# A third PSUM bank for the cross products of batch 0, 33 rows of bias, and the last two units ahead of the splits

## The chip, the cores and the metric

The kernel runs on one core of a Trainium2 chip. Its time is device microseconds of one execution; a comparison uses the median of several. Before the change the median of 3 runs is 2718.03 us (2716.43 to 2720.4). The engines are called PE (TensorE), DVE (VectorE), ACT (ScalarE), POOL (GpSimd) and SP (SyncE, which here only issues DMAs). PSUM is the memory that PE writes its results to; this kernel divides it into eight banks of 128 x 512 float32.

## What is computed

A spectral layer (a real Fourier transform along the sequence, a complex linear map with a soft threshold, the inverse transform) and then a feed-forward layer on all 8 x 3008 rows:

```python
X = np.fft.rfft(x, axis=1)                    # x is (8, 3008, 256)
Yr = Xr @ w_r - Xi @ w_i + b_r
Yi = Xr @ w_i + Xi @ w_r + b_i
lam = 0.01
Yr = np.sign(Yr) * np.maximum(np.abs(Yr) - lam, 0.0)
Yi = np.sign(Yi) * np.maximum(np.abs(Yi) - lam, 0.0)
y = np.fft.irfft(Yr + 1j * Yi, n=3008, axis=1)
h = y.reshape(8 * 3008, 256) @ w_in           # (256, 2048)
out = (h - np.tanh(h)) @ w_out                # (2048, 256)
```

## The kernel before

**The transforms.** The length 3008 is 64 x 47, so a transform is two stages of matmuls. Forward: `Forward` (a chunk of 4 of the 32 row pairs) computes the 47-point stage and writes its result to a DRAM tile `a`; `Spectrum` (a pair of the 24 frequency columns, 12 pairs a batch) reads `at` back, does the 64-point stage (`transform`), the complex product with the linear weights (`cross`), the soft threshold and the first inverse stage (`inverse`), and writes `zo` to a DRAM tile `z` (`put`). `Chunk` (5 row pairs, 470 columns) reads `zin` back from `z`, does the second inverse stage (`time`, in two halves) and the feed-forward layer in 16 steps, `up` (tiles `h`, `th`, `g`, `gh`, `gl`) and `down` (`o`). To keep float32 precision most matmuls are done on a high and a low part (`split`), three products each.

**Batch 0 is done alone.** Nothing of the feed-forward layer can start until batch 0's `z` is there, so batch 0 has a version of its own, with whole float32 matmuls in place of three products: `WholeSpectrum`, whose twelve instances are the `units` u0 to u11. A unit's steps:

- `dft`: the 64-point stage on PE (L288) and ACT's copy `xf` (L360). `sum`: `sf` on DVE (L365).
- `cross`: three pairs of matmuls on PE. Two go to `vv` (`ps_v`), behind a matmul that puts the biases there (`ones` by `brow`, 33 rows, L370); the third, the part that both results share, goes to `t1` (`ps_t`).
- `common`: ACT copies `t1` to `tb` (L380). `shrink`: DVE adds `tb` and `vv` to `y` in four pieces (L333), ACT does one side of the threshold (`up`, L385), DVE the other (`mn`, L387). `join`: DVE adds the two (L391).
- `inverse`: PE's matmul to `pz` (L395). `put`: ACT's copy `zo` (L350) and the DMA of `z`.

In the loop over the units, iteration i does the `dft` of unit i, `cross` of unit i-1, `common`, `shrink` and `join` of unit i-2, and `inverse` and `put` of unit i-3. Beside them it loads the weights of the feed-forward layer, which come in float64, and converts them on DVE, ACT and POOL (`convert`, a list `ops` of which each iteration takes some), and reads the constant `i2t` of the second inverse stage. The chunks of batch 1's forward transform that follow (`following`, four of them) and `time` of the first two feed-forward chunks are written out by hand behind the loop.

**What sets the order.** All of this stands in a `manual_schedule` for the five engines: each engine executes its instructions in the order in which the code issues them, and waits at each for what it needs. Behind it come the feed-forward steps, one slot each; a plan (`put`, `plan_forward`, `plan_spectrum`) sets into which slot a step of the next batch's transforms goes.

**PSUM.** The pool `ps_h` has two banks (`h`, and in the units' part `ps_v`), `ps_o` two (tags `o0` and `o1`, in the units' part `ps_t1`), `ps_f` four for the rest. A tile can be written when the tile that had the bank before it has been read. `keep_warm` issues matmuls on zeros to a tile `idle` of `ps_h`, which nothing reads; it is called with 8 at the start and with 16 ahead of the units.

**Bias.** `load_linear` loads the two weight matrices and the tile `bias`, each bias row to all 128 partitions. `combine_linear` makes `brow` from 33 of its rows; `bias` itself is read again in batches 1 to 7 (L322).

Of the kernel before, what the change touches and what calls it, by code (L numbers as in the profile page):

```python
# [10 lines left out]
F32 = mybir.dt.float32  # L11
# [5 lines left out]
B, S, D, FF = 8, 3008, 256, 2048  # L17
# [51 lines left out]
def spectral_ffn(ctx, tc, x, w_r, w_i, b_r, b_i, w_in, w_out, f1, f2, i1, i2, out):  # L69
    nc = tc.nc  # L70
    P = 128
# [8 lines left out]
    const = ctx.enter_context(tc.tile_pool(name="const", bufs=1))  # L80
    load = ctx.enter_context(tc.tile_pool(name="load", bufs=2))
    work = ctx.enter_context(tc.tile_pool(name="work", bufs=2))
# [24 lines left out]
    def load_linear():  # L107
        wr = ffn.tile([P, 2, D], F32, name="wr_f", tag="g_h")
        wi = load.tile([P, 2, D], F32, name="wi_f", tag="at", bufs=3)
        nc.sync.dma_start(out=wr, in_=w_r.rearrange("(t p) e -> p t e", p=P))  # L110
        nc.sync.dma_start(out=wi, in_=w_i.rearrange("(t p) e -> p t e", p=P))
        bias = const.tile([P, 2, D], F32, name="bias")
        for k, v in enumerate((b_r, b_i)):
            nc.sync.dma_start(out=bias[:, k, :], in_=v.rearrange("(o e) -> o e", o=1).to_broadcast([P, D]))
        return wr, wi, bias

    def combine_linear(wr, wi, bias, zero):
        w2 = ffn.tile([P, 2, D], F32, name="w2_f", tag="g_h")
        w3 = ffn.tile([P, 2, D], F32, name="w3_f", tag="g_h")
        nc.vector.scalar_tensor_tensor(out=w3, in0=wr, scalar=-1.0, in1=wi, op0=ALU.mult, op1=ALU.subtract)  # L120
        nc.gpsimd.tensor_tensor(out=w2, in0=wi, in1=wr, op=ALU.subtract)
        ones = work.tile([33, P], F32R, name="ones", tag="s_l")
        nc.vector.tensor_scalar(out=ones, in0=zero[:33, :P], scalar1=1.0, scalar2=None, op0=ALU.add)
        top = work.tile([33, 2 * D], F32R, name="bias_top", tag="tmp", bufs=4)
        flat = bias[:33].rearrange("o r e -> o (r e)")
        nc.scalar.copy(out=top, in_=flat)  # L126
        brow = work.tile([33, 2 * D], F32R, name="brow", tag="ot", bufs=1)
        nc.vector.tensor_copy(out=brow, in_=zero[:33])
        nc.vector.tensor_copy(out=brow[0:1], in_=top[0:1].bitcast(F32))
        nc.vector.tensor_tensor(out=brow[32:33], in0=flat[32:33], in1=top[32:33].bitcast(F32), op=ALU.subtract)  # L130
        return (wr, w2, w3), (ones, brow)
# [136 lines left out]
    class Spectrum:  # L268
# [79 lines left out]
        def put(self, pz):  # L348
            zo = work.tile([P, 512], F32, name="zo", tag="tmp", bufs=4)
            nc.scalar.copy(out=zo, in_=pz)  # L350
            nc.sync.dma_start(out=z_rows(z_dram[self.b], self.jp), in_=zo)

    class WholeSpectrum(Spectrum):
        def temp(self, name, tag):
            return ffn.tile([P, 2, D], F32, name=name, tag=tag)
# [9 lines left out]
            nc.vector.tensor_tensor(out=self.sf, in0=pr[:, :, 0, :], in1=self.xf[:, :, 1, :], op=ALU.add)  # L365

        def cross(self):
            self.vv = ps_h.tile([P, 512], F32, name="ps_v", tag="h")
            ones, brow = bias_rows
            nc.tensor.matmul(self.vv, ones, brow, start=True, stop=False)  # L370
            self.t1 = ps_o.tile([P, 512], F32, name="ps_t1", tag=f"o{self.jp % 2}")
            for k, (dst, lhs) in enumerate((
                (self.vv[:, :D], self.xf[:, :, 1]), (self.vv[:, D:], self.xf[:, :, 0]), (self.t1[:, :D], self.sf),
            )):
                for t in range(2):
                    nc.tensor.matmul(dst, lhs[:, t], whole_lin[2 - k][:, t, :], start=k == 2 and t == 0, stop=k > 0 and t == 1)

        def common(self):
            self.tb = work.tile([P, D], F32, name="tb0", tag="xi")
            nc.scalar.copy(out=self.tb, in_=self.t1[:, :D])  # L380

        def shrink(self):
            y = self.add(lambda jj, ri: self.tb[jj * 64:(jj + 1) * 64, :])
# [94 lines left out]
    def plan_forward(b, start, each, ahead, first=0):  # L478
        for ch in range(first, NP // XC):
            f = Forward(b, ch)  # L480
            put(start + ch * each - ahead, f.load)
            for q in range(XC // 2):
                put(start + ch * each + q * each // 2, f.part, q)

    def plan_spectrum(b, start, each, ahead, lag):
        for jp in range(NJ // 2):
            s = Spectrum(b, jp)
            at = start + jp * each
            put(at - ahead, s.load)
            put(at, s.dft)  # L490
            put(at + lag, s.cross, 0)
            put(at + lag + 1, s.cross, 1)
            put(at + lag + 2, s.shared)
            put(at + 2 * lag + 3, s.inverse)
# [5 lines left out]
    chunks = [Chunk(c) for c in range(NCH)]  # L500
# [6 lines left out]
    with tc.manual_schedule(engines={E.PE, E.Activation, E.DVE, E.Pool, E.SP}):  # L507
# [6 lines left out]
        def keep_warm(n):  # L514
            for _ in range(n):
                nc.tensor.matmul(idle, warm[:, :P], warm, start=True, stop=True)
# [14 lines left out]
                f, q = steps[i - 1]  # L531
                f.keep(q, nc.vector.tensor_copy if i % 2 == 0 else nc.scalar.copy)
        lin_in = load_linear()
        bias = lin_in[2]
        keep_warm(16)
        units = [WholeSpectrum(0, jp) for jp in range(NJ // 2)]
        for u in units[:3]:
# [6 lines left out]
        raws, ops = [], []  # L544
# [10 lines left out]
        def unit(i):  # L555
            return units[i] if 0 <= i < NU else None

        for i in range(NU + 1):
            if unit(i - 2):
                unit(i - 2).common()  # L560
            if unit(i):
# [14 lines left out]
            if i < len(where):  # L576
# [2 lines left out]
                    nc.sync.dma_start(out=i2t[:, :10 * 94], in_=i2[:, :10 * 94])  # L579
                if i % 2:  # L580
                    ops += convert([(k // 4, k % 4, raws[k]) for k in (i - 1, i)])
            if i == 7:
                nc.sync.dma_start(out=i2t[:, 10 * 94:], in_=i2[:, 10 * 94:])
            if i in (8, 9):
                following[i - 8].load()
            if 3 <= i < 6:
                split_lin(i - 3)
            for op in ops[:(0, 0, 2, 2, 2, 2, 2, 3, 3, 3, 3, 2, 0)[i]]:
                op()
                ops.remove(op)  # L590
            if i in (11, 12):
                following[0].split(i - 11)
        assert not ops
        u10, u11 = units[-2:]
        LATE = 80
        following[2].load()
        for c in range(2):
            chunks[c].load(0, LATE)
        u10.inverse()
        for q in range(2):  # L600
            following[0].dft(q)
        u11.common()
        u11.shrink()
        u10.put(u10.pz)
        u11.join()
        u11.inverse()
        following[1].split(0)
        following[0].keep(0, nc.vector.tensor_copy)
        u11.put(u11.pz)
        for c in range(2):  # L610
            chunks[c].load(LATE, 96)
        following[0].keep(1)
        following[3].load()
        following[1].dft(0)
        following[1].split(1)
        following[1].keep(0, nc.vector.tensor_copy)
        following[1].dft(1)
        following[2].split(0)
        following[1].keep(1)
        following[2].dft(0)  # L620
        following[2].split(1)
        following[2].keep(0, nc.vector.tensor_copy)
        following[2].dft(1)
        for t in range(2):
            chunks[0].time(t)
        following[2].keep(1)
        for q in range(2):
            following[3].split(q)
            following[3].dft(q)
            following[3].keep(q, (nc.scalar.copy, nc.vector.tensor_copy)[q])  # L630
        for t in range(2):
            chunks[1].time(t)

    for i in range(2):
        put(2 * i - 2, ffn_weights, 1, 2 + i)
    for i in range(8):
        put(1 + 8 * i // 3, ffn_weights, 2 + i // 4, i % 4)
    plan_forward(1, 8, 2, 3, LOOK)
    plan_spectrum(1, 31, 4, 7, 2)
    for b in range(2, B):  # L640
        end = NF * (next(c for c in range(NCH) if begin[c] + sizes[c] > b * NP) - 1)
        plan_forward(b, end - 104, 2, 3)
# [48 lines left out]
```

## Time and profile before

| what | us |
|---|---|
| median of 3 runs | 2718.03 |
| the profiled execution's own time | 2716.88 |
| its span | 2715.1 |
| PE busy | 2679.6 |
| DVE busy | 1733.3 |
| ACT busy | 1380.0 |
| POOL busy | 56.6 |

The span runs from the first instruction to the last of one profiled execution; the time has 1.8 us around it. From 200 to 2500 us PE is idle for 1.6 us in all; the first 200 us hold batch 0 and the first feed-forward steps. In the views below, a row of a timeline is: start in us, duration in us, engine, line, operation, the tile written and the tiles read, with a count where several of one kind follow each other, and in brackets the idle time of the engine ahead of it and what ended it. A row of the chain that ended last is start, duration and what.

### The profile page before, as it was taken

How to read it: one execution, taken by the hardware profiler on the slowest of the kernel's cores; microseconds unless marked ns; L12 is line 12 of the kernel's file. 1: busy time of each engine (PE TensorE's matmuls, PEld its weight loads, DVE VectorE, ACT ScalarE, POOL GpSimd, SP SyncE). 2: the span in 40 equal slices, each digit the busy share in tenths (PEclk: the TensorE clock that was granted, in tenths of full speed). 3: DMA queues.
4: the chain of work that ended last, by engine and by line, in shares of the span. 5: the costliest groups of instructions: out<-in, count | busy, mean ns of one | idle time of the engine just before them, and what ended most of it. 6: DMA issues, size and time to landing. Idle time of an engine off the chain costs nothing.

```text
span 2715.1 us, 36888 instructions
## 1 busy us (share of the span) xinstructions
PE 2679.6 (99%) x14112; PEld 2385.1 (88%) x14112; DVE 1733.3 (64%) x3041; ACT 1380.0 (51%) x2591; POOL 56.6 (2%) x47
## 2 busy tenths in 40 slices
PE   8799999999999999999999999999999999999999
PEld 5579888999889998899988999899988999998989
DVE  5786776766556666567665666656675667655555
ACT  3584455444554455545455454645446444444445
POOL 2130000000000000000000000000000000000000
PEclk9899999999999999999999999999999999999999
DMA  7532114111131113211023110311104111100000
GB/s 209 154 110 66 46 59 118 42 49 36 41 110 49 38 36 101 70 46 49 28 58 101 38 53 31 107 59 46 48 24 121 45 42 40 35 22 22 20 19 17
DMA packets 105217, 163.58 MB, mean 60 GB/s; under 512 B 7440, under 2 KB 71056, under 8 KB 104944
## 3 DMA queue, kind: packets, MB, share of 16 engines
q1 hardware_dynamic: 105040, 161.22, 19.8%
q8 instruction: 111, 1.82, 0.3%
q14 instruction: 66, 0.54, 0.1%
HBM read 86.22 MB, written 74.97 MB: 59 GB/s over the span
## 4 chain that ended last, share of the span: by engine, by line
PE 92%; DVE 4%; ACT 1%; DMA 1%; issue 1%; POOL 0%; SPq 0%; DVEq 0%; ACTq 0%; POOLq 0%
PE o L460 37%; PE h L439 36%; PE ps_v L308 4%; PE ps_i L426 4%; PE ps_f L288 3%; PE ps_t L308 2%; DVE y L333 1%; PE ps_f L236 1%; PE ps_f L238 1%; PE ps_f L237 1%; PE ps_i L344 1%; PE ps_i L345 1%; PE ps_i L343 1%; DVE g L444 0%; DMA a<-st 0%
## 5 line engine op out<-in xcount | busy, mean ns | idle before, releaser
L444 DVE TENSOR_TENSOR g<-h,th 128x470 f32<-128x470 f32 (+1 forms) x832 | 531.7, 639 | 560.5 <-ACT th L442 552.7
L442 ACT ACTIVATE th<-h 128x470 f32<-128x470 f32 (+1 forms) x832 | 462.9, 557 | 768.4 <-PE h L439 768.2
L448 DVE TENSOR_TENSOR gl<-g,gh 128x470 fp32r<-128x470 f32 (+1 forms) x832 | 533.2, 641 | 289.2 <-ACT gh L446 203.3
L446 ACT CAST gh<-g 128x470 fp32r<-128x470 f32 (+1 forms) x832 | 482.8, 580 | 390.5 <-DVE g L444 382.3
L460 PE MATMUL o<-gh,wout_l 128*128 128x470 f32 (+1 forms) x1664 | 632.4, 380 | 1.4 <-ACT gh L446 1.3
L460 PE MATMUL o<-gl,wout_h 128*128 128x470 f32 (+1 forms) x1664 | 616.5, 371 | 3.5 <-DVE gl L448 3.4
L460 PE MATMUL o<-gh,wout_h 128*128 128x470 f32 (+1 forms) x1664 | 615.7, 370 | 0.0
L439 PE MATMUL h<-yh,win_l 128*128 128x470 f32 (+1 forms) x1664 | 481.5, 370 | 4.3 <-DVE g L444 3.8
L439 PE MATMUL h<-yl,win_h 128*128 128x470 f32 (+1 forms) x1664 | 480.7, 370 | 0.0
L439 PE MATMUL h<-yh,win_h 128*128 128x470 f32 (+1 forms) x1664 | 480.6, 370 | 0.0
L460 PEld LDWEIGHTS o<-gl,wout_h 128*128 128x128 f32 x1664 | 312.9, 188 | 45.1 <-DVE gl L448 6.4
L439 PEld LDWEIGHTS h<-yh,win_l 128*128 128x128 f32 x1664 | 310.7, 188 | 41.8 <-DVE g L444 4.7
L460 PEld LDWEIGHTS o<-gh,wout_l 128*128 128x128 f32 x1664 | 313.0, 188 | 36.5 <-issue 1.8
L439 PEld LDWEIGHTS h<-yh,win_h 128*128 128x128 f32 x1664 | 311.0, 188 | 35.6
L439 PEld LDWEIGHTS h<-yl,win_h 128*128 128x128 f32 x1664 | 310.9, 188 | 35.6
L460 PEld LDWEIGHTS o<-gh,wout_h 128*128 128x128 f32 x1664 | 313.5, 188 | 32.0
L333 DVE TENSOR_TENSOR y<-tb,ps_v 64x256 f32<-64x256 f32 x384 | 160.0, 417 | 13.0 <-ACT tb L380 9.0
L426 PEld LDWEIGHTS ps_i<-i,zin 96*128 96x128 f32 x1024 | 128.3, 194 | 4.4 <-issue 1.3
L426 PE MATMUL ps_i<-i,zin 96*128 96x94 f32 x1024 | 130.0, 275 | 0.6 <-DMA zin<-z 0.6
L288 PEld LDWEIGHTS ps_f<-f,at 128*128 128x128 f32 x768 | 101.1, 192 | 13.8 <-issue 8.8
L288 PE MATMUL ps_f<-f,at 128*128 128x128 f32 x768 | 102.8, 276 | 6.2 <-ACT bias_top L126 6.2
L94 DVE TENSOR_TENSOR x_l<-xt,x_h 94x512 fp32r<-94x512 f32 x112 | 78.6, 708 | 46.4 <-ACT x_h L93 46.3
(102 smaller groups left out, 2102.3 us busy)
## 6 DMA issues: line engine op xcount, KB each, us to landing
xt<-in_x SPq DMA_DIRECT2D x64, 384.0 KB, 3.7
at<-a SPq DMA_DIRECT2D x96, 256.0 KB, 2.8
z<-zo SPq DMA_DIRECT2D x96, 256.0 KB, 2.4
out<-ot SPq DMA_DIRECT2D x50, 470.0 KB, 3.0
a<-st SPq DMA_DIRECT2D x56, 384.0 KB, 3.2
zin<-z SPq DMA_DIRECT2D x42, 480.0 KB, 4.1
w_raw<-in_moe_w_in SPq DMA_DIRECT2D x8, 512.0 KB, 4.3
w_raw<-in_moe_w_out SPq DMA_DIRECT2D x8, 512.0 KB, 3.9
```

What stands on the lines that cost most here:

```text
L94: rest.tensor_tensor(out=lo, in0=src, in1=hi.bitcast(F32), op=ALU.subtract)
L236: nc.tensor.matmul(pv, f1h, xl, start=True, stop=False)
L288: nc.tensor.matmul(pv[:, t, jj], self.at[:, jj, t * P:(t + 1) * P], rhs, start=True, stop=True)
L308: nc.tensor.matmul(dst, lhs[:, t], rhs[:, t, :], start=n == 0, stop=n == 5)
L333: nc.vector.tensor_tensor(out=y[ri * 64:(ri + 1) * 64, jj, :], in0=common(jj, ri), in1=self.vv[jj * 64:(jj + 1) * 64, ri * D:(ri + 1) * D] ...
L426: nc.tensor.matmul(ps[:, k * 94:(k + 1) * 94], self.zt[:, k, t * P:(t + 1) * P], i2t[:, p * 94:(p + 1) * 94], start=True, stop=True,)
L439: nc.tensor.matmul(h[:, :n], lhs[:, t, f * P:(f + 1) * P], rhs[:, t, :n], start=k == 0, stop=k == 5)
L442: nc.scalar.activation(out=th[:, :n], in_=h[:, :n], func=AF.Tanh)
L444: nc.vector.tensor_tensor(out=g[:, :n], in0=h[:, :n], in1=th[:, :n], op=ALU.subtract)
L446: nc.scalar.copy(out=gh[:, :n], in_=g[:, :n])
L448: nc.vector.tensor_tensor(out=gl[:, :n], in0=g[:, :n], in1=gh[:, :n].bitcast(F32), op=ALU.subtract)
L460: nc.tensor.matmul(self.o[t][:, :n], lhs[:, f, t * P:(t + 1) * P], rhs[:, :n], start=f == 0 and k == 0, stop=f == NF - 1 and k == 2,)
```

## The change

- `load_linear` loads the bias rows to 33 partitions only, as a tile `bias_rows` that `combine_linear` reads. The tile `bias` for 128 partitions is loaded later, by `load_bias(bias, P)` behind the loop.
- `vv` of every third unit (u2, u5, u8, u11) comes from the bank `o1`. `t1` of two units shares one tile, in two halves of the bank `o0`.
- The loop ends one iteration earlier, and what is left of u9, u10 and u11 is written out: `shrink`, `cross`, `join`, `inverse` and `put` of these stand ahead of the splits of `following[0]`, with a `keep_warm(7)` between them. The weight conversions that are left over (`ops`) stand behind `dft` and `keep` of `following[1]`.
- The second part of `i2t` is loaded there and not in iteration 7. The `dft` of `following[2]` stands behind `time` of the first feed-forward chunk.
- In the plan for batch 1, the forward chunks start at slot 12 and not 8, the spectra at 35 and not 31, with 11/3 slots each and not 4.

The built programs differ in the banks as well as in the order. `idle` is written again by `keep_warm(7)`, so it has its bank of `ps_h` until then, and the units' `ps_v` have one bank of `ps_h` and `o1`: u0 and u1 the bank of `ps_h`, u2 `o1`, u3 and u4 the bank of `ps_h`, u5 `o1`, and so on. Before, the `ps_v` have both banks of `ps_h` in turn, and `ps_t` both of `ps_o`.

PE's rows in iterations 8 and 9, with the engines that a row's first instruction waits for, before (`ps_v` of u7 is the first of them, `ps_t_617` is its `t1`, `ps_i_625` is the inverse of u5, `ps_f_644` the dft of u9, and the last row is `ps_v` of u8):

```order
L370 MATMUL ps_v<-brow,ones 128x512 [waits DVE_49,PE_49]
L376 MATMUL ps_v<-w_f,xf 128x256 [waits Activation_49]
L376 MATMUL ps_v<-w_f,xf 128x256 x3
L376 MATMUL ps_t_617<-wr_f,sf 128x256 [waits DVE_49]
L376 MATMUL ps_t_617<-wr_f,sf 128x256
L395 MATMUL ps_i_625<-mn,i_f 128x512 [waits DVE_49,PE_49]
L288 MATMUL ps_f_644<-f_131,at 128x2x64 [waits DMAHW3_49,PE_49]
L288 MATMUL ps_f_644<-f_131,at 128x2x64 x3
L370 MATMUL ps_v<-brow,ones 128x512 [waits DVE_49,PE_49]
```

And the same place now:

```order
L378 MATMUL ps_v<-brow,ones 128x512 [waits DVE_49,PE_49]
L386 MATMUL ps_v<-w_f,xf 128x256 [waits Activation_49]
L386 MATMUL ps_v<-w_f,xf 128x256 x3
L386 MATMUL ps_t_569<-wr_f,sf 128x256 [waits Activation_49]
L386 MATMUL ps_t_569<-wr_f,sf 128x256
L405 MATMUL ps_i_621<-mn,i_f 128x512
L291 MATMUL ps_f_640<-f_131,at 128x2x64 [waits DMAHW3_49]
L291 MATMUL ps_f_640<-f_131,at 128x2x64 x3
L378 MATMUL ps_v<-brow,ones 128x512
```

The order is the same; the waits moved. `ps_v` of u7 waits for DVE in both: before for y of u5, now for y of u6, which had the bank. `ps_v` of u8 (last row) waits for DVE before and for nothing now. `t1` of u7 waits now for ACT, which copies `t1` of u6 out of the same bank.

ACT's rows at the end of the units, before (the first `zo` is that of u8, `tb_775` is of u10, `tb_821` of u11, the last `zo` is that of u11):

```order
L350 COPY zo<-ps_i_760 128x512
L187 CAST win_h<-w_f 128x512 x2
L93 CAST x_0_0_h<-xt 94x512
L380 COPY tb_775<-ps_t_752 128x256
L385 ACTIVATE up<-y,column 128x512
L350 COPY zo<-ps_i_796 128x512
L93 CAST x_0_1_h<-xt 94x512
L380 COPY tb_821<-ps_t_788 128x256
L385 ACTIVATE up<-y,column 128x512
L350 COPY zo<-ps_i_811 128x512
L93 CAST x_1_0_h<-xt 94x512
L350 COPY zo<-ps_i_836 128x512
```

And now (`tb_760` is of u10, `tb_782` of u11):

```order
L353 COPY zo<-ps_i_755 128x512
L390 COPY tb_760<-ps_t_747 128x256
L395 ACTIVATE up<-y,column 128x512
L390 COPY tb_782<-ps_t_747 128x256
L353 COPY zo<-ps_i_780 128x512
L395 ACTIVATE up<-y,column 128x512
L353 COPY zo<-ps_i_796 128x512
L93 CAST x_0_0_h<-xt 94x512
L93 CAST x_0_1_h<-xt 94x512
L353 COPY zo<-ps_i_813 128x512
```

The two casts `win_h` and the splits of `following[0]` and `following[1]` (`x_0_0_h` to `x_1_0_h`) stood between the steps of u10 and u11; now only the two of `following[0]` stand there, ahead of the last `zo`.

PE's rows around `time` of the first feed-forward chunk (`ps_i_889`, `ps_i_897`), before:

```order
L236 MATMUL ps_f_883<-x_2_1_l,f_h 96x512
L237 MATMUL ps_f_883<-x_2_1_h,f_l 96x512
L238 MATMUL ps_f_883<-x_2_1_h,f_h 96x512
L426 MATMUL ps_i_889<-i_265,zin 128x94 x5
L426 MATMUL ps_i_897<-i_265,zin 128x94 x5
L439 MATMUL h<-yh,win_l 128x470 x2
```

And now:

```order
L436 MATMUL ps_i_875<-i_266,zin 128x94 x5
L436 MATMUL ps_i_883<-i_266,zin 128x94 x5
L449 MATMUL h<-yh,win_l 128x470 x2
L449 MATMUL h<-yh,win_h 128x470 x2
L449 MATMUL h<-yl,win_h 128x470 x2
L239 MATMUL ps_f_895<-x_2_0_l,f_h 96x512
L240 MATMUL ps_f_895<-x_2_0_h,f_l 96x512
L241 MATMUL ps_f_895<-x_2_0_h,f_h 96x512
```

The forward stage of `following[2]` (`x_2_0`, `x_2_1`) stood ahead of `time`; it now stands behind the first `h`.

The diff:

```diff
@@ -109,12 +109,15 @@
         nc.sync.dma_start(out=wi, in_=w_i.rearrange("(t p) e -> p t e", p=P))
-        bias = const.tile([P, 2, D], F32, name="bias")
+        rows = load_bias(work.tile([33, 2, D], F32, name="bias_rows", tag="tmp", bufs=4), 33)
+        return wr, wi, rows
+
+    def load_bias(dst, n):
         for k, v in enumerate((b_r, b_i)):
-            nc.sync.dma_start(out=bias[:, k, :], in_=v.rearrange("(o e) -> o e", o=1).to_broadcast([P, D]))
-        return wr, wi, bias
-
-    def combine_linear(wr, wi, bias, zero):
+            nc.sync.dma_start(out=dst[:, k, :], in_=v.rearrange("(o e) -> o e", o=1).to_broadcast([n, D]))
+        return dst
+
+    def combine_linear(wr, wi, rows, zero):
         w2 = ffn.tile([P, 2, D], F32, name="w2_f", tag="g_h")
@@ -122,7 +125,7 @@
         top = work.tile([33, 2 * D], F32R, name="bias_top", tag="tmp", bufs=4)
-        flat = bias[:33].rearrange("o r e -> o (r e)")
+        flat = rows.rearrange("o r e -> o (r e)")
         nc.scalar.copy(out=top, in_=flat)
@@ -350,6 +353,8 @@
+    t1_pair = []
+
     class WholeSpectrum(Spectrum):
@@ -365,19 +370,24 @@
         def cross(self):
-            self.vv = ps_h.tile([P, 512], F32, name="ps_v", tag="h")
+            if self.jp % 3 < 2:
+                self.vv = ps_h.tile([P, 512], F32, name="ps_v", tag="h")
+            else:
+                self.vv = ps_o.tile([P, 512], F32, name="ps_v", tag="o1")
             ones, brow = bias_rows
             nc.tensor.matmul(self.vv, ones, brow, start=True, stop=False)
-            self.t1 = ps_o.tile([P, 512], F32, name="ps_t1", tag=f"o{self.jp % 2}")
+            if self.jp % 2 == 0:
+                t1_pair.append(ps_o.tile([P, 2, D], F32, name="ps_t1", tag="o0"))
+            self.t1 = t1_pair[-1][:, self.jp % 2]
             for k, (dst, lhs) in enumerate((
-                (self.vv[:, :D], self.xf[:, :, 1]), (self.vv[:, D:], self.xf[:, :, 0]), (self.t1[:, :D], self.sf),
+                (self.vv[:, :D], self.xf[:, :, 1]), (self.vv[:, D:], self.xf[:, :, 0]), (self.t1, self.sf),
             )):
...
             self.tb = work.tile([P, D], F32, name="tb0", tag="xi")
-            nc.scalar.copy(out=self.tb, in_=self.t1[:, :D])
+            nc.scalar.copy(out=self.tb, in_=self.t1)
@@ -485,7 +495,7 @@
             s = Spectrum(b, jp)
-            at = start + jp * each
+            at = start + int(jp * each)
             put(at - ahead, s.load)
@@ -531,7 +541,7 @@
         lin_in = load_linear()
-        bias = lin_in[2]
+        bias = const.tile([P, 2, D], F32, name="bias")
         keep_warm(16)
@@ -555,7 +565,7 @@
-        for i in range(NU + 1):
+        for i in range(NU):
             if unit(i - 2):
@@ -579,64 +589,69 @@
                     ops += convert([(k // 4, k % 4, raws[k]) for k in (i - 1, i)])
-            if i == 7:
-                nc.sync.dma_start(out=i2t[:, 10 * 94:], in_=i2[:, 10 * 94:])
             if i in (8, 9):
...
                 split_lin(i - 3)
-            for op in ops[:(0, 0, 2, 2, 2, 2, 2, 3, 3, 3, 3, 2, 0)[i]]:
+            for op in ops[:(0, 0, 2, 2, 2, 2, 2, 3, 3, 3, 3, 0)[i]]:
                 op()
                 ops.remove(op)
-            if i in (11, 12):
-                following[0].split(i - 11)
-        assert not ops
-        u10, u11 = units[-2:]
+        u9, u10, u11 = units[-3:]
         LATE = 80
-        following[2].load()
+        u10.common()
+        u10.shrink()
+        u11.cross()
+        u10.join()
+        u9.inverse()
+        u11.common()
+        u9.put(u9.pz)
+        u11.shrink()
+        u10.inverse()
+        keep_warm(7)
         for c in range(2):
             chunks[c].load(0, LATE)
-        u10.inverse()
-        for q in range(2):
-            following[0].dft(q)
-        u11.common()
-        u11.shrink()
         u10.put(u10.pz)
...
         u11.inverse()
+        for q in range(2):
+            following[0].split(q)
+        u11.put(u11.pz)
+        following[2].load()
+        chunks[0].load(LATE, 96)
+        nc.sync.dma_start(out=i2t[:, 10 * 94:], in_=i2[:, 10 * 94:])
+        chunks[1].load(LATE, 96)
+        for q in range(2):
+            following[0].dft(q)
         following[1].split(0)
-        following[0].keep(0, nc.vector.tensor_copy)
-        u11.put(u11.pz)
-        for c in range(2):
-            chunks[c].load(LATE, 96)
+        following[0].keep(0)
+        following[1].split(1)
         following[0].keep(1)
         following[3].load()
-        following[1].dft(0)
-        following[1].split(1)
-        following[1].keep(0, nc.vector.tensor_copy)
-        following[1].dft(1)
-        following[2].split(0)
-        following[1].keep(1)
-        following[2].dft(0)
-        following[2].split(1)
-        following[2].keep(0, nc.vector.tensor_copy)
-        following[2].dft(1)
+        load_bias(bias, P)
+        for q in range(2):
+            following[1].dft(q)
+            following[1].keep(q)
+        for op in ops:
+            op()
         for t in range(2):
             chunks[0].time(t)
-        following[2].keep(1)
+        for q in range(2):
+            following[2].split(q)
+            following[2].dft(q)
+            following[2].keep(q, (nc.scalar.copy, nc.vector.tensor_copy)[q])
+        for t in range(2):
+            chunks[1].time(t)
         for q in range(2):
...
             following[3].keep(q, (nc.scalar.copy, nc.vector.tensor_copy)[q])
-        for t in range(2):
-            chunks[1].time(t)
...
         put(1 + 8 * i // 3, ffn_weights, 2 + i // 4, i % 4)
-    plan_forward(1, 8, 2, 3, LOOK)
-    plan_spectrum(1, 31, 4, 7, 2)
+    plan_forward(1, 12, 2, 3, LOOK)
+    plan_spectrum(1, 35, 11 / 3, 7, 2)
     for b in range(2, B):
```

## The prediction

> **What bounds the kernel now.** I read the page's first line, then the windows (us, then busy time and instructions of PE, PEld, DVE, ACT and POOL, granted clock, DMA share, GB/s).
>
> ```profile
> span 2715.1 us, 36888 instructions
> ```
>
> ```profile
> 64.00:98.00 34.00, 29.41 (x131) 21.62 (x129) 29.76 (x67) 19.43 (x37) 10.75 (x10) 1.00 0.43 129
> 118.50:200.00 81.50, 72.33 (x329) 59.11 (x329) 66.94 (x102) 64.41 (x119) 27.76 (x20) 0.98 0.46 128
> 500.00:1000.00 500.00, 500.00 (x2676) 450.97 (x2676) 323.69 (x570) 251.41 (x473) 0.00 (x0) 1.00 0.17 52
> ```
>
> From 500 to 1000 PE is never idle, so whatever the change does there costs only if it adds matmuls, and it adds none. The change can be worth something only in the first 200 us. In the loop over the whole-precision units (64 to 98) PE is idle for 4.59 of 34 us while DVE is busy for 29.76: there the pace is set by DVE and ACT, and PE has slack. The waits (us in total, times, longest) name the edge that the third bank is aimed at:
>
> ```profile
> PE ps_v L370 <- DVE y L333: 4.5, 6, 1.2
> ```
>
> That is 4.5 us in six waits, on an engine that is not the bound there. Removing them all would give less than 4.5.
>
> **The third bank, part by part.** Units are u0 to u11. Iteration i issues to PE the dft of u(i), the cross products of u(i-1), the inverse of u(i-3); y of u(i-2) runs on DVE at the same time. In the changed program `keep_warm(7)`, behind the loop, writes `idle` again, so `idle` keeps its bank of `ps_h` until then. `ps_v` of u0, u1 stands in one bank and u2 in the third, u3 and u4 in the first again, and so on; all pairs of `t1` share one bank. So u1, u4, u7 and u10 wait for y of the unit just ahead of them, which is y of their own iteration, where before a unit waited for y of two units ahead; u2, u5, u8 and u11 do not wait. Each `t1` waits for tb of the unit just ahead. The bank is moved, not added.
>
> What such a wait holds up is read at iteration 8, in ACT's timeline, then PE's (start, us, engine, line, operation):
>
> ```profile
> 77.62 0.56 ACT L350 COPY zo<-ps_i 128x512 f32<-128x512 f32 x1
> 79.71 1.22 ACT L187 CAST wout_h<-w_f 128x512 fp32r<-128x512 f32 x2 [1.53 <-DVE w_f L186]
> 80.83 0.37 ACT L380 COPY tb<-ps_t 128x256 f32<-128x256 f32 x1
> ```
>
> ```profile
> 79.33 1.03 PE L376 MATMUL ps_t<-wr_f,sf 128*128 128x256 f32 x4
> 80.19 1.02 PE L395 MATMUL ps_i<-mn,i_f 128*128 128x512 f32 x2
> ```
>
> And the four pieces of y on DVE at the places that matter:
>
> ```profile
> 40.76 1.71 DVE L333 TENSOR_TENSOR y<-tb,ps_v 64x256 f32<-64x256 f32 x4 [5.22 <-ACT tb L380]
> ...
> 57.53 1.71 DVE L333 TENSOR_TENSOR y<-tb,ps_v 64x256 f32<-64x256 f32 x4
> ...
> 75.24 1.72 DVE L333 TENSOR_TENSOR y<-tb,ps_v 64x256 f32<-64x256 f32 x4 [0.62 <-ACT tb L380]
> ...
> 91.91 1.71 DVE L333 TENSOR_TENSOR y<-tb,ps_v 64x256 f32<-64x256 f32 x4
> ```
>
> y ends at 76.96, and in this iteration the cross products follow it even before; the inverse ends at 81.21, 4.25 later. So zo, which takes this inverse's result, can start 4.3 after y's end in the changed kernel. Before, zo took a result already there and started at 77.62, 0.66 after y. ACT runs in order: the casts and the next tb stand behind zo.
>
> - Iteration 8: zo at 81.26, done 81.82, casts 1.22 behind it with little between, tb at 82.9 or so in place of 80.83: **+2.05**.
> - Iteration 5: y (57.53) ends 59.24, zo at 63.54 and behind it the cast of w_h and two of win_h, about 1.5 us, so tb at 65.6. Before:
>
> ```profile
> 63.60 0.36 ACT L380 COPY tb<-ps_t 128x256 f32<-128x256 f32 x1
> ```
>
>  **+2.0**.
> - Iteration 11: y ends 93.62, zo at 97.92 and before at 94.29, with nothing left in between to hide it: **+3.6**.
>
> ```profile
> 94.29 0.56 ACT L350 COPY zo<-ps_i 128x512 f32<-128x512 f32 x1
> ```
>
> - Iteration 2: cross products before at 41.14, while y0 ends at 42.47, so PE stands for 1.3; ACT and DVE are not yet behind, and I take **+0.8**.
>
> ```profile
> 41.14 0.50 PE L370 MATMUL ps_v<-brow,ones 33*128 33x512 f32 x1
> ```
>
> Sum +8.4. Its bounds: nothing, if ACT and DVE catch up each time before the next such wait; +13, if each costs the whole 3.6 (4.3 less 0.66) but the first 1.3 (3 x 3.6 + 1.3 = 12.1, and 1 for the later `t1` waits).
>
> **The clock.** Before, PE's 4.59 idle us lie scattered. With two units of three that wait for nothing, they gather ahead of the third: per three iterations (y from 57.53 to 75.24 is 17.71, to 91.91 is 16.67) PE is idle for 17.2 x 4.59 / 34 = 2.3, and the 2 us that the wait adds make 4.3 in one piece. What short idle stretches did to the clock, in windows on a grid of 3.413 us:
>
> ```profile
> 32.91:36.33 3.42, 3.42 (x12) 2.58 (x11) 0.85 (x2) 1.06 (x2) 0.00 (x0) 0.50 0.74 212
> 36.33:39.74 3.41, 3.41 (x10) 2.69 (x9) 0.00 (x0) 0.00 (x0) 0.00 (x0) 0.50 0.97 301
> 90.94:94.35 3.41, 2.18 (x8) 1.06 (x7) 3.27 (x8) 2.07 (x5) 1.39 (x1) 1.00 0.14 53
> 97.77:101.18 3.41, 0.11 (x1) 0.00 (x0) 3.01 (x7) 1.24 (x4) 1.64 (x1) 1.00 0.00 0
> 101.18:104.59 3.41, 3.04 (x5) 1.61 (x6) 3.01 (x7) 1.18 (x3) 0.00 (x0) 0.52 0.52 154
> 108.01:111.42 3.41, 1.77 (x6) 0.81 (x6) 1.91 (x4) 2.12 (x4) 0.00 (x0) 1.00 0.70 217
> 111.42:114.83 3.41, 2.19 (x7) 1.23 (x6) 0.67 (x1) 0.00 (x0) 0.00 (x0) 0.52 0.38 100
> ```
>
> A window with PE busy for 0.11 and one with 1.77 were followed by half the clock; one with 2.18 was not (the clock of 64 to 98 is 1.00 throughout). A gap of 4.3 lies on the grid so that one window holds at least 2.15 of it, that is, PE busy at most 1.27: each of the three late gaps (ahead of u4, u7, u10) is followed by half clock. One window of it costs at most half its work, 3.41 / 2 = 1.7, and waits that fall differently put an estimate at 1.4 to 2.4; I take 1.9 each, **+5.7**. At 32.91 two full windows in a row ran at half: two each time would make 3.4 to 3.6 each. Bounds: 0 to 10.8. [...]
>
> **The front.** The bias rows go to 33 partitions in place of 128. One transfer (KB, us to landing) and PE's first dft in the chain that ended last (start, us):
>
> ```profile
> bias<-in_b_i SPq DMA_DIRECT2D x1, 128.0 KB, 6.1
> ```
>
> ```profile
> 30.71 3.75 PE ps_f L288 x16
> ```
>
> Both transfers stand on SP's queue ahead of `at` and the dft waits for `at`. Of 256 rows of 1 KB, 190 go. At 300 GB/s or so that this queue moves (301 in the row of 36.33) 190 KB are 0.65 us; by the landing, three quarters of 6.1 would be 4.6, but both overlap others. I take **-1.5**, bounds -0.3 and -3.
>
> **The tail.** Behind the loop the chains of u10 and u11 come ahead of the splits and the last conversions. Lengths, where they last ran:
>
> ```profile
> 104.16 0.72 ACT L385 ACTIVATE up<-y,column 128x512 f32<-128x512 f32 x1 [2.23 <-DVE y L333]
> ...
> 104.92 0.69 DVE L391 TENSOR_TENSOR mn<-up,mn 128x512 f32<-128x512 f32 x1 [0.33 <-ACT up L385]
> ...
> 105.76 1.10 PE L395 MATMUL ps_i<-mn,i_f 128*128 128x512 f32 x2 [0.19 <-DVE mn L391]
> ...
> 106.93 0.58 ACT L350 COPY zo<-ps_i 128x512 f32<-128x512 f32 x1 [1.06 <-issue]
> ```
>
> ```profile
> 107.54 4.38 DMA z<-zo
> ```
>
> Before, 107.54 - 94.29 = 13.25 pass from zo of u8 to the last z write. After: zo .56, tb .37, y 1.71, up .72, tb .37, y 1.71, up .72, join .69, inverse 1.10, zo .58 = 8.5, with steps between about 9.15: **-4.1**. Bounds: -5 and -2 (PE may be at half clock there, 1.1 more, and `up` may queue behind zo). `keep_warm(7)` runs in the gap between the two inverses, where PE waits for DVE; without that gap it would cost at most 7 x 0.50 = 3.5 (512 columns each, by the row of 41.14). The z writes now stand ahead of `following[2].load` on SP, the second part of `i2t` behind the first reads of z: that can take or give 1, and I take 0.
>
> **Behind the tail.** The conversions and the splits of `following[1]` move behind the chains, and the dft of `following[2]` behind `time(0)`:
>
> ```profile
> 142.50 0.40 PE L236 MATMUL ps_f<-x_l,f_h 94*96 94x512 f32 x1
> ```
>
> From 118.5 to 200 PE is idle for 9.2 of 81.5, so most of what is moved there fills gaps; six matmuls of at most 0.40 are 2.4 at worst, and DVE and ACT (66.94 and 64.41 of 81.5 busy) take up the rest. I take **+1**, bounds -3 and +3. The later slots of batch 1 (8 to 12, 31 to 35) and the bias load for 128 rows that only batch 1 reads cost nothing: PE is full there, and the order of full work does not change its sum (bounds -0.5, +0.5).
>
> **Sum:** -1.5 + 8.4 + 5.7 - 4.1 + 0 + 1 = +9.5. The profiled execution took 2716.88 (span 2715.1 and 1.8 around it); +9.5 gives 2726.4. The median shown, 2718.03, is 1.15 above it: **2727.5**.
>
> **Rivals.**
> 1. The clock holds, as a gap of 2.3 with 2.18 busy did: -1.5 + 8.4 - 4.1 + 1 = +3.8, **2721.8**. For it: the gaps may be split by the eight matmuls of the next dft, which wait for nothing. Against it: the 1.77 row. [...]
> 2. The change does what it says: the waits are hidden, since DVE, which sets the pace, works on conversions while PE waits: -1.5 - 4.1 + 1 = -4.6, **2713.4**. This is the other side, not slower. It decides where zo's lag of 3.6 stays under the slack of ACT; for it speaks that ACT is busy only 19.43 of 34, against it that tb stands behind zo and y behind tb.
> 3. Half clock for two windows each time, as at 32.91: -1.5 + 8.4 + 10.8 - 4.1 + 1 = +14.6, **2732.6**.
>
> **How the numbers follow.** Forecast 0.62 (its own range 2723.5 to 2731), rival 1 0.18, rival 2 0.10, rival 3 0.10. The range 2717.5 to 2733 leaves out rival 2 and part of rival 3 with little above. 0.2%, about what a measurement of this kernel can tell from no change, is 5.4 us: faster needs under 2712.6, about half of rival 2 (0.06 with the lower ends of rival 1); within 0.2% are rival 1, the rest of rival 2 and some of the forecast's low end: 0.28; slower 0.66.
>
> **What would show it.** Right: PE's wait for y ahead of `ps_v` rises from 4.5 to 13 or more in four waits, three of them 4 to 5 long; half clock behind each; zo 4.3 behind the end of y in iterations 5, 8 and 11; the last z write leaves about 9.2 behind zo of u8; first dft near 29.2. Wrong: a loop that keeps 5.5 us an iteration, clock 1.00 from 64 to 98, or an end that moves by more behind 200 than ahead of it.

## The result, and the profile after

| | before | changed |
|---|---|---|
| median of 5 runs, us | 2718.03 (2716.43 to 2720.4) | 2732.59 (2731.59 to 2733.81) |
| ratio | | 1.0054, 95% interval 1.0039 to 1.0069 |
| span of the profiled execution, us | 2715.1 | 2729.8 |

The change makes the kernel 14.6 us slower. The difference is split below into five stretches, read from the chain that ended last (start, us, what) and ACT's timeline. The chain of the changed kernel:

```profile
28.10 3.75 PE ps_f L291 x16
...
116.94 6.02 DMA z<-zo
123.02 2.30 DMA zin<-z
125.36 4.59 PE ps_i L436 x20
```

And the one row of the chain of before that the prediction did not show:

```profile
114.30 4.56 PE ps_i L426 x20
```

ACT's timeline of the changed kernel, where y of u3 ends (`up` starts) and where `zo` of u2, u5 and u8 start:

```profile
58.20 0.72 ACT L395 ACTIVATE up<-y,column 128x512 f32<-128x512 f32 x1 [1.31 <-DVE y L336]
65.58 0.59 ACT L353 COPY zo<-ps_i 128x512 f32<-128x512 f32 x1 [6.66 <-PE ps_i L405]
...
81.58 0.72 ACT L395 ACTIVATE up<-y,column 128x512 f32<-128x512 f32 x1 [1.29 <-DVE y L336]
87.46 0.59 ACT L353 COPY zo<-ps_i 128x512 f32<-128x512 f32 x1 [5.17 <-PE ps_i L405]
...
101.81 0.72 ACT L395 ACTIVATE up<-y,column 128x512 f32<-128x512 f32 x1 [1.31 <-DVE y L336]
107.73 0.59 ACT L353 COPY zo<-ps_i 128x512 f32<-128x512 f32 x1 [5.19 <-PE ps_i L405]
```

| stretch, us | before | changed | difference | forecast |
|---|---|---|---|---|
| start to the first dft of the units | 30.71 | 28.10 | -2.6 | -1.5 |
| from there to `zo` of u8 (the loop) | 63.58 | 79.63 | +16.05 | +14.1 |
| from there to the last z write (the tail) | 13.25 | 9.21 | -4.0 | -4.1 |
| from there to the second inverse stage | 6.76 | 8.42 | +1.7 | 0 |
| from there to the end | 2600.80 | 2604.44 | +3.6 | +1 |
| sum | 2715.10 | 2729.80 | +14.7 | +9.5 |

The loop carries all of the loss; the two gains and the two smaller losses nearly cancel. The waits of the changed kernel (us in total, times, longest) show the edge that the third bank was to remove, three times as large as before, and behind it ACT standing for the inverse:

```profile
ACT zo L353 <- PE ps_i L405: 21.9, 9, 6.7
...
PE ps_v L378 <- DVE y L336: 14.1, 4, 4.9
```

In PE's timeline it is four waits, the first of 1.4 and then these, ahead of u4, u7 and u10 (the idle time and what ended it stand in brackets):

```profile
58.31 0.76 PE L378 MATMUL ps_v<-brow,ones 33*128 33x512 f32 x1 [4.15 <-DVE y L336]
...
81.69 0.65 PE L378 MATMUL ps_v<-brow,ones 33*128 33x512 f32 x1 [4.88 <-DVE y L336]
...
101.93 0.47 PE L378 MATMUL ps_v<-brow,ones 33*128 33x512 f32 x1 [3.68 <-DVE y L336]
```

The clock falls behind each of these three waits. In short windows of this profile it changes at 57.92, 64.75, 81.81, 85.22, 102.29 and 105.70, points that lie whole multiples of 3.413 us apart. In the kernel before it changes at other points (101.34, 104.75, 111.58 and 121.82 among them), so the edges of the prediction's windows do not hold for this execution. These are the windows on its own edges, the one ahead of each fall first (columns as in the prediction; the clock is the third number from the right):

```profile
54.51:57.92 3.41, 0.00 (x0) 0.00 (x0) 3.34 (x8) 1.84 (x4) 1.45 (x1) 1.00 0.82 250
57.92:61.33 3.41, 3.02 (x7) 2.17 (x8) 2.89 (x6) 0.72 (x1) 0.00 (x0) 0.50 0.14 58
61.33:64.75 3.42, 3.42 (x9) 2.66 (x8) 0.00 (x0) 0.00 (x0) 0.00 (x0) 0.50 0.00 0
78.40:81.81 3.41, 0.12 (x1) 0.15 (x1) 2.72 (x8) 1.61 (x4) 1.26 (x1) 1.00 0.39 117
81.81:85.22 3.41, 3.41 (x8) 2.44 (x9) 3.02 (x6) 0.49 (x1) 0.00 (x0) 0.50 0.00 0
85.22:88.64 3.42, 3.42 (x17) 2.45 (x16) 0.00 (x0) 1.18 (x3) 0.00 (x0) 1.00 0.00 0
98.88:102.29 3.41, 0.36 (x1) 0.18 (x1) 3.27 (x9) 1.85 (x4) 1.39 (x1) 1.00 0.20 77
102.29:105.70 3.41, 3.41 (x9) 2.76 (x9) 1.00 (x2) 0.25 (x1) 0.00 (x0) 0.50 0.00 0
105.70:109.12 3.42, 3.42 (x13) 2.18 (x13) 0.49 (x2) 0.86 (x2) 0.00 (x0) 1.00 0.00 0
```

PE is idle for nearly the whole window ahead of each fall (0.00, 0.12 and 0.36 us busy). Half clock then lasts for two windows, one and one, and the cross products and the inverse that everything waits for run in it. While PE does them, ACT and DVE run out of work: in the last window of each of the three groups DVE is busy for 0.00 to 0.49 us and ACT for 0.00 to 1.18.

### The profile page after: what moved, and what is told of

Its sections match the earlier page's. It is cut to its first block, busy times and chain, and to the rows that moved or that the text cites. A ratio compares the mean times of both kernels' runs of the same rounds, so it can differ in the third digit from the quotient of the medians.

```text
span 2729.8 us, 36908 instructions
## 1 busy us (share of the span) xinstructions
PE 2685.7 (98%) x14119; PEld 2390.3 (88%) x14119; DVE 1733.4 (63%) x3039; ACT 1384.1 (51%) x2593; POOL 56.0 (2%) x47
## 4 chain that ended last, share of the span: by engine, by line
PE 94%; DVE 3%; ACT 1%; DMA 1%; issue 1%; SPq 0%; POOL 0%; DVEq 0%; ACTq 0%; POOLq 0%
PE o L470 37%; PE h L449 37%; PE ps_v L311 4%; PE ps_i L436 4%; PE ps_f L291 3%; PE ps_t L311 2%; PE ps_f L239 1%; PE ps_f L241 1%; PE ps_f L240 1%; PE ps_v L386 1%; DVE y L336 1%; PE ps_i L347 1%; PE ps_i L348 1%; PE ps_i L346 1%; DMA a<-st 0%
```

## The experiments

The theory: `keep_warm(7)` holds the bank of `idle`, so the third bank is none; four units wait for y of their own iteration; and the gaps cost twice, by the wait and by the clock behind it. Rivals: the shared bank of `t1` or the order of the tail makes the loop slow; the clock costs nothing. Times below are against the kernel before in the same comparison (its medians were 2718.03 beside the changed kernel, then 2717.04, 2716.18 and 2716.16).

| kernel | median, us | minus before, us | ratio, 95% interval |
|---|---|---|---|
| changed | 2732.59 | +14.6 | 1.0054 (1.0039 to 1.0069) |
| e1_own_tile | 2713.21 | -3.8 | 0.9987 (0.9978 to 0.9996) |
| e3_idle_held | 2753.57 | +36.5 | 1.0143 (1.0127 to 1.0158) |
| e4_third_bank | 2717.98 | +0.9 | 1.0003 (0.9994 to 1.0012) |
| e5_bias_rows | 2716.56 | -0.5 | 1.0002 (0.9993 to 1.0011) |
| e9_warm_gaps | 2723.14 | +7.0 | 1.0023 (1.0014 to 1.0032) |
| e2_no_late_warm | 2714.29 | -1.9 | 0.9991 (0.9982 to 1.0000) |
| e8_bias_in_slot | 2714.85 | -1.3 | 0.9992 (0.9984 to 1.0001) |
| e10_warm_z | 2711.38 | -4.8 | 0.9977 (0.9967 to 0.9986) |
| e6_own_tile_old_banks | 2714.29 | -1.9 | 0.9992 (0.9983 to 1.0001) |
| e7_old_plan | 2714.73 | -1.4 | 0.9993 (0.9984 to 1.0002) |
| e11_warm_both | 2711.31 | -4.9 | 0.9975 (0.9965 to 0.9984) |

**A tile of its own for the late warming.** One line of the changed kernel:

```diff
-        def keep_warm(n):
+        def keep_warm(n, idle=idle):
...
-        keep_warm(7)
+        keep_warm(7, ps_f.tile([P, 512], F32, name="idle2", tag="f"))
```

> Changed kernel, but keep_warm(7) writes a tile of its own (from ps_f), so that idle gives its bank of ps_h back before the units. If the held bank is the cause: no waits of ps_v for y, no gaps of 4 to 5 us ahead of u4, u7 and u10, granted clock 1.00 from the second unit to the last, and zo of u8 about 16 us earlier against the first dft; time 2732.6 - 16 = 2716.6 (2714 to 2719). If instead the shared bank of t1 or the order of the tail makes the loop slow: the loop stays long, time over 2727.

2713.21, a little below the 2714 to 2719 expected: the loss of 14.6 is gone and 3.8 of gain stands in its place. The loop takes 64.58 us, where the changed kernel took 79.63. In its waits `ps_v` waits for y no more; what is left in the loop is `t1` waiting for tb of the unit ahead, and the window of 64 to 98 has the full clock (0.94 in the changed kernel):

```profile
PE ps_t L386 <- ACT tb L390: 2.7, 3, 1.2
```

```profile
64.00:98.00 34.00, 31.72 (x135) 22.05 (x134) 30.54 (x70) 18.72 (x36) 7.84 (x6) 1.00 0.30 94
```

The shared bank of `t1` and the order of the tail are the same here as in the changed kernel, so neither is the cause. `warm`, which the late matmuls read, keeps its buffer as long in both, so it is not that either.

**The held bank alone.** The kernel before, with one matmul to `idle` behind the loop:

```diff
         LATE = 80
+        keep_warm(1)
         following[2].load()
```

> Kernel before, with one more matmul to idle behind the loop and nothing else, so that idle holds its bank and all ps_v stand in one bank of ps_h. If the held bank is the cause: every unit's cross products wait for y of the unit ahead, an iteration goes from 5.3 to about 8 us (tb .4, y 1.7, cross products 2.9, inverse 1.1, zo .6, casts 1.2 to 2), so +25 to +35 in ten iterations: 2740 to 2755. If the late use of idle does not matter: 2718 (one matmul more, 0.2).

One matmul costs 36.5 us, at the upper end. All `ps_v` have one bank, each unit waits, and here too the clock falls (0.84 from 64 to 98):

```profile
PE ps_v L370 <- DVE y L333: 32.4, 11, 4.8
```

```profile
64.00:98.00 34.00, 24.12 (x88) 17.95 (x86) 15.26 (x34) 11.25 (x22) 6.41 (x6) 0.84 0.29 86
```

**The third bank alone.** The kernel before with the changed `cross` and `common`:

```diff
-            self.vv = ps_h.tile([P, 512], F32, name="ps_v", tag="h")
+            if self.jp % 3 < 2:
+                self.vv = ps_h.tile([P, 512], F32, name="ps_v", tag="h")
+            else:
+                self.vv = ps_o.tile([P, 512], F32, name="ps_v", tag="o1")
...
-            self.t1 = ps_o.tile([P, 512], F32, name="ps_t1", tag=f"o{self.jp % 2}")
+            if self.jp % 2 == 0:
+                t1_pair.append(ps_o.tile([P, 2, D], F32, name="ps_t1", tag="o0"))
...
```

> Kernel before, with the changed cross products alone (third bank for ps_v, t1 in pairs; idle is not used late, so its bank is free). Theory: the six waits of ps_v for y (4.5 us) go, but DVE and ACT set the pace, so the time moves by under 1.5: 2716.5 to 2719. Rival, that the waits were on the path: -4.5, 2713.5. Rival, that t1 in one bank costs (PE waits for tb of the unit ahead): over 2720.

With the bank free the six waits of 4.5 us are gone and the time is the same; the loop takes 63.74 us, before 63.58. But four new waits stand in their place: `ps_t` waits for tb, for 4.3 us in all. That the six waits were hidden is argued from DVE's share of the loop (29.29 of 34 us busy here); this run does not tell it apart from the new waits taking back what the old ones gave.

**The bias rows alone.** The kernel before with `load_bias` for 33 rows, and the full load behind `following[3].load()`:

```diff
-        bias = const.tile([P, 2, D], F32, name="bias")
+        rows = load_bias(work.tile([33, 2, D], F32, name="bias_rows", tag="tmp", bufs=4), 33)
...
         following[3].load()
+        load_bias(bias, P)
```

> Kernel before, with the bias rows loaded to 33 partitions and the full load behind the loop. Theory: the first dft starts 2.6 us earlier, as in the changed kernel, and all of it is kept: 2715.4 (2714.5 to 2716.5). Rival: the loop, which DVE paces later, or the later load gives it back: 2717.5 to 2718.5.

No difference that can be measured; 2716.56 lies between the two forecasts. The one profile shows a gain, and that it is gone at the end: the first dft starts 1.9 us earlier than before and the second inverse stage 4.3, yet the span ends only 0.5 earlier (2714.6).

```profile
28.80 3.42 PE ps_f L291 x16
...
109.96 4.57 PE ps_i L429 x20
```

That the 4.3 are more than the 1.9 goes with the clock: in this execution the half clock at the start of the units was over by 31.7, before only by 39.9. Behind the z write PE then stood at half clock from 106.8 to 123.9, 17 us, and before from 111.6 to 121.8, 10 us. How much of the lost gain that is, these two executions do not show.

**Full clock with the waits kept.** The changed kernel, with matmuls that yield nothing in the three long gaps:

```diff
             if unit(i - 1):
+                if i > 2 and i % 3 == 2:
+                    keep_warm(12)
                 unit(i - 1).cross()
```

> Changed kernel, with 12 matmuls to idle (no result) ahead of the cross products of u4, u7 and u10, which fill 2.6 us of the gaps of 4.1, 4.9 and 3.7 us while PE waits for y anyway; waits and banks as in the changed kernel. If the half clock behind the gaps costs what the profile of the changed kernel shows (zo 7.4, 5.9 and 6.0 behind the end of y in place of 4.3, together 6.3), the clock stays at 1.00 from u3 to u10 and the time is 2732.6 - 6.3 = 2726 (2725 to 2728). If the clock costs nothing and the wait is all: 2732 to 2734.

+7.0 in place of +14.6, a little better than the 2725 to 2728 expected: 7.6 us of the loss were the clock. What is left of it holds the waits, less what the tail gains. The profile agrees: the loop takes 73.19 us, which is 6.4 less than in the changed kernel (the clock) and 9.6 more than before (the waits). ACT's timeline has `zo` 4.3 us behind the end of y (59.02 - 0.03), as worked out for full clock:

```profile
59.02 0.72 ACT L395 ACTIVATE up<-y,column 128x512 f32<-128x512 f32 x1 [1.30 <-DVE y L336]
63.28 0.58 ACT L353 COPY zo<-ps_i 128x512 f32<-128x512 f32 x1 [3.54 <-PE ps_i L405]
```

The windows show no fall behind the gaps, again on the execution's own edges (its clock falls at 28.00, 116.75 and 147.47):

```profile
55.31:58.72 3.41, 2.44 (x11) 1.67 (x9) 3.34 (x8) 1.89 (x4) 1.46 (x1) 1.00 0.82 256
58.72:62.14 3.42, 3.01 (x13) 2.51 (x14) 2.92 (x6) 0.72 (x1) 0.00 (x0) 1.00 0.13 52
75.79:79.20 3.41, 1.49 (x7) 0.90 (x5) 2.72 (x8) 1.38 (x3) 1.26 (x1) 1.00 0.47 151
79.20:82.62 3.42, 3.21 (x14) 2.69 (x15) 3.31 (x7) 0.72 (x1) 0.00 (x0) 1.00 0.00 0
96.27:99.68 3.41, 2.50 (x11) 1.68 (x10) 3.01 (x7) 1.05 (x2) 1.12 (x1) 1.00 0.02 5
99.68:103.09 3.41, 3.41 (x14) 2.18 (x13) 0.03 (x1) 0.86 (x2) 0.00 (x0) 1.00 0.00 0
```

**Without the late warming.** The changed kernel less one line:

```diff
-        keep_warm(7)
```

> Changed kernel without keep_warm(7): idle is free as with a tile of its own. Theory: as e1_own_tile, 2713 (2711.5 to 2715). If the seven matmuls hold up the clock for the last inverse and what follows: 1 to 2 more than e1_own_tile, 2714 to 2716.

-1.9, which the intervals do not tell from -3.8: the seven matmuls are worth nothing that can be measured, and it is their tile that cost.

**Where the rest behind the second inverse stage goes.** The stretch from the second inverse stage to the end is 3.6 us longer in the changed kernel. Two variants of e1_own_tile were to find why, and a third takes the banks back. The late bias load in slot 14:

```diff
-        load_bias(bias, P)
...
+    put(14, load_bias, bias, P)
```

> e1_own_tile, with the full load of the bias rows moved from behind the loop to slot 14 of the plan. In e1_own_tile the second inverse stage starts 4.6 us earlier than before but the span ends only 1.0 earlier. If the late bias load ahead of the conversions' weight loads on SP's queue is what gives 3.6 back: 2710 (2709 to 2711.5). If the conversions on DVE and ACT (or the clock) give it back: 2712.5 to 2714.

The plan of before:

```diff
-    plan_forward(1, 12, 2, 3, LOOK)
-    plan_spectrum(1, 35, 11 / 3, 7, 2)
+    plan_forward(1, 8, 2, 3, LOOK)
+    plan_spectrum(1, 31, 4, 7, 2)
```

> e1_own_tile with batch 1's plan of before (slots 8 and 31, 4 each). Theory: PE is full in those slots and the plan is worth nothing: 2712 to 2714.5. If the later plan costs part of the 3.6 that the span loses behind the second inverse stage: 2710 to 2711.5; if it saves: 2715 or more.

The banks of before, with the tile of its own kept:

```diff
-            if self.jp % 3 < 2:
-                self.vv = ps_h.tile([P, 512], F32, name="ps_v", tag="h")
-            else:
-                self.vv = ps_o.tile([P, 512], F32, name="ps_v", tag="o1")
+            self.vv = ps_h.tile([P, 512], F32, name="ps_v", tag="h")
...
+            self.t1 = ps_o.tile([P, 512], F32, name="ps_t1", tag=f"o{self.jp % 2}")
...
```

> e1_own_tile with the banks of before for ps_v and t1 (no third bank, no shared tile): what is left is the bias rows, the reordered tail and the plan. Theory: the third bank hides waits that were hidden anyway, so the time is that of e1_own_tile, 2713 (0.9980 to 0.9995 of before). If the third bank, once it is one, carries the gain: 2716 to 2718.

-1.3, -1.4 and -1.9, with intervals that hold e1_own_tile's ratio of 0.9987 and that all three just reach 1. None of the three parts can be told from nothing; the first two medians lie just above what was expected, the third inside it. In their profiles the stretch behind the second inverse stage takes 2605.5, 2605.4 and 2605.1 us, in e1_own_tile 2604.4: neither the late load nor the plan gives back the 3.6, and the third bank, once it is one, carries no gain that shows.

The two profiles of the change show where the 3.6 stands. In that stretch PE is busy for 1.25 us more (2587.16 and 2585.91; six matmuls of `following[2]` moved into it) and idle for 2.4 more. The idle time is gathered in the 20 us that start 20 us into it, where PE waits for g and gl of DVE, and DVE, with the conversions that are left over, is busier than before. Before, then changed:

```profile
134.30:154.30 20.00, 18.71 (x86) 15.44 (x86) 17.07 (x29) 17.47 (x33) 8.37 (x7) 1.00 0.45 120
145.36:165.36 20.00, 13.46 (x56) 9.60 (x54) 18.81 (x27) 15.20 (x28) 10.66 (x7) 1.00 0.45 129
```

No run puts the conversions or the moved matmuls back, so that they are the cause is not shown.

**Warming across the z transfer.** e1_own_tile with 16 matmuls ahead of `chunks[0].time`:

```diff
         for op in ops:
             op()
+        keep_warm(16, ps_f.tile([P, 512], F32, name="idle3", tag="f"))
         for t in range(2):
             chunks[0].time(t)
```

> e1_own_tile, with 16 more matmuls to a tile of its own ahead of the second inverse stage of chunk 0, where PE is idle for 4.8 us while z is written and read back. If half clock behind that gap is on the path, the second inverse stage takes 2.4 in place of 4.6 and the first steps less: 2713.2 - 2 to - 5, 2708 to 2711. If the conversions on DVE and ACT set the pace there: 2712.5 to 2714.

-4.8 against before, faster than both kernels, and just above the 2708 to 2711 expected. In e1_own_tile PE is idle for 4.8 us while z is written and read back, and the second inverse stage runs at half clock (0.50 in the windows from 108.01 to 114.84):

```profile
109.69 4.58 PE L436 MATMUL ps_i<-i,zin 96*128 96x94 f32 x20 [4.83 <-DMA zin<-z]
```

With the warming it takes 2.4 us, at a granted clock of 1.00 (104.60 to 111.42):

```profile
101.32 3.83 PE L526 MATMUL idle<-warm 128*128 128x512 f32 x16
105.90 2.44 PE L436 MATMUL ps_i<-i,zin 96*128 96x94 f32 x20 [0.74 <-issue]
```

In the profiles the stretch from the second inverse stage to the end takes 2601.2 us in place of 2604.4. Against e1_own_tile itself the step in time is 1.0 us by the differences to the kernel before and 2.7 by the ratios, where 2 to 5 were forecast; the two intervals overlap (0.9967 to 0.9986 and 0.9978 to 0.9996), so its size stays open.

**Warming ahead of the units too.**

```diff
-        keep_warm(16)
+        keep_warm(28)
         units = [WholeSpectrum(0, jp) for jp in range(NJ // 2)]
```

> e10_warm_z with 28 matmuls in place of 16 ahead of the units, which fill 3 of the 3.8 us in which PE waits for the first at. If the half clock at the start of the units (up to 8 us in the runs so far) is on the path: 1 to 4 less than e10_warm_z, 2707 to 2710. If DVE's pace in the loop takes it back: 2711 to 2712.

2711.31, the same as e10_warm_z and not the 2707 to 2710 expected. In its profile PE finished the first dft sooner and then waited 3.1 us for `xf`, behind a cast on ACT that waits for the load of `i1`; the clock was at half from 32.9 to 39.7 all the same:

```profile
33.40 0.30 ACT L93 CAST i_h<-i_f 128x128 fp32r<-128x128 f32 x1 [5.31 <-DMA i_f<-in_i]
```

## Why the prediction was right

The forecast was 2727.5, slower; measured was 2732.6. That is at the top of the range of 2717.5 to 2733 and above the 2723.5 to 2731 that the forecast gave itself. The mechanism is the one that the forecast named. Its terms missed by -1.1 (front), +1.95 (loop), +0.1 (tail), +1.7 (z transfer) and +2.6 (the rest), so more than half of the 5.2 us missed has nothing to do with that mechanism.

- **The held bank: right, and shown by taking it away and by adding it alone.** The four waits came where they were expected (u1, u4, u7, u10), 14.1 us in all. e1_own_tile takes 18.4 us off (from +14.6 to -3.8), e3_idle_held puts 36.5 on the kernel before by the same cause. That the changed cross products gain nothing when the bank is free is shown by e4_third_bank; that this is so because the old waits were hidden is argued, since four waits for tb came in their place.
- **The clock: right, and a little under-sized.** `zo` starts 7.4, 5.9 and 6.0 us behind the end of y (65.58 - 58.16, 87.46 - 81.55, 107.73 - 101.78): 4.3 is the wait, and 3.1, 1.6 and 1.7 the clock, 6.4 in all for the +5.7 of the sum. The loop of e9_warm_gaps gives the same 6.4; the times make it 7.6 (14.6 less 7.0), with an interval of several us. One window of half clock cost no more than the 1.7 that the prediction worked out as its most; the 1.9 that it then took is above that bound. The sum is low because the first fall lasted two windows. This was neither one window throughout nor the two of rival 3 each time. In the windows ahead of the three falls PE was busy for 0.00, 0.12 and 0.36 us; each gap was followed by half clock, so rival 1 falls. In the kernel before a fuller window was followed by it too: its row of 1.77 is 1.85 on its own edges (108.17 to 111.58).
- **The waits themselves: right in place, under-sized.** The loop's +16.05 less 6.4 is 9.7, and e9_warm_gaps has 9.6 with the clock kept, where the sum had +8.4.
- **The tail: right to 0.1.** 9.21 where 9.15 was forecast, and 9.21 again in e9_warm_gaps.
- **The bias rows: the first dft came 2.6 us sooner, where 1.5 was taken; but alone they are worth nothing that shows** (e5_bias_rows). The reading that the first dft waits for `at` was not quite right: by the profile before, `at` landed at 30.00, and what released the dft at 30.71 was the cast `bias_top` (0.62 us) behind it. Now `at` lands at 27.97 and the dft follows it at 28.10, the cast being done. The step that failed is to carry the gain at the front over to the end in full: in the profile of e5_bias_rows 4.3 us of gain at the second inverse stage are 0.5 at the end, beside a longer stretch of half clock.
- **Behind the tail: the two terms that were mis-sized.** The z transfer was put at 0 and cost +1.7 (the landing 6.02 in place of 4.38). But this landing took 4.49 and 5.32 in e5_bias_rows and e4_third_bank, which have the tail of before, and 4.51 to 5.99 in others with the new tail, so part of it may be one execution against another. The stretch behind it was put at +1, at most +3, and took +3.6: 1.25 of more work for PE and 2.4 of more waiting for DVE. That DVE and ACT would take up what was moved is the assumption that did not hold there. It is no chance of one execution: that stretch took 2604.0 to 2605.7 in six other kernels with this order and no warming across the z transfer, and 2602.3 and 2602.6 in e4_third_bank and e3_idle_held with the order of before (2604.6 in e5_bias_rows, with its longer half clock).
- **Rival 2, the change as it was meant,** was worked out at -4.6. e1_own_tile, which is that, measured -3.8 (-6.0 to -1.1 by its interval). It did not decide here because the bank was not free. **Rival 3** gives 2732.6, the measured time to 0.1, by luck: the clock's share was 6.4 and not 10.8, and the rest came from the terms above.

## What to carry to other kernels

A tile keeps its bank until its last use in the program: a late write to an old scratch tile can take the buffer from a whole loop (in e3_idle_held one late matmul raised the waits of `ps_v` for y from 4.5 to 32.4 us and the time by 36.5), so after a change to buffers look at which tile waits for which in the built order, not at the count in the pool. Removing waits that lay scattered on an engine with slack gained nothing here (six waits of 4.5 us in e4_third_bank, +0.9); the same idle time gathered in one piece can cost its length and then the clock (9.7 and 6.4 us in the loop of the changed kernel). Matmuls without a result in a gap that must stay gave part of it back: 7.6 of the 14.6 us in e9_warm_gaps.

## What the runs showed of the hardware that was not expected

- In each of the 13 profiles the granted clock changes only at points a whole multiple of 3.413 us apart (29.66, 39.90, 101.34, 104.75, 111.58 and 121.82 in the kernel before and 28.00, 38.24, 116.75 and 126.99 in e9_warm_gaps, for example), and these points lie elsewhere in each execution. So windows have to be cut at the execution's own edges. Cut so, over the first 200 us of all profiles, each of the 30 windows at full clock with PE busy for 1.39 us or less was followed by half clock, though most of them were not wholly idle. Between 1.43 and 2.14 both happened (1.85 in the kernel before fell, 1.49 in e9_warm_gaps did not), and above that none fell.
- How long half clock lasts differs as much as whether it comes: behind z it was 10 us in the kernel before and 17 in e5_bias_rows, which has the same matmuls there. A busy window did not always end it: in the kernel before PE was busy for all of 114.99 to 118.41 and the clock stayed at half until 121.82.
- The spread of the runs of the kernel before goes with the clock. Of its 25 runs beside e6_own_tile_old_banks, the nine with a mean granted clock of 0.993 took 2717.22 to 2719.15 us, the eight with 0.996 took 2713.96 to 2715.65.
